# Gate values of a feed-forward layer, rounded and subtracted by single blocks or by pairs, beside block-sparse attention on one core

## The chip, the cores and the metric

The kernel runs on one core of a Trainium2 chip. The metric is the time of one execution in device microseconds (us); less is better. The engines work in parallel, each through its own instructions in a fixed order: TensorE (PE, matmuls into PSUM banks), VectorE (DVE), ScalarE (ACT), GpSimd (POOL) and SyncE (SP, which here issues nearly all DMA transfers).

## The reference

Attention with a block mask over 4 batches of 8 heads (768 positions, 64 columns a head), then a feed-forward layer with a piecewise gate, all in fp32:

```
scores = scale * q @ k.T                     # (B, H, S, S), masked to -1e9 outside chosen 32x32 blocks
attn   = softmax(scores) ;  a = attn @ v
x = a.transpose(0, 2, 1, 3).reshape(3072, 512)
h = x @ w_in                                 # 512 -> 2048
g = where(h >= 1, h, where(h <= -1, 0, (h + 1)**2 / 4))
out = g @ w_out                              # 2048 -> 512
```

## The kernel before

**Numbers.** Matmuls run on values in a rounded format (F32R). For near fp32 accuracy an operand is split into a rounded part "hi" and the rest "lo" = value - hi, and a product is made of three matmuls: hi*hi, hi*lo, lo*hi. So each gate value `r` needs a rounding cast (`gh`, on ACT) and a subtraction (`gl`, on DVE).

**Attention.** Each head works through scores (L318, L319), exponentials (L323, ACT), their rounding `ph` (L196, ACT) and rest `pl` (L331, DVE), and the products with v (L350, L351). Beside these run the row maxima of the next head (L267 on PE, L272 on DVE).

**Feed-forward.** `moe` works on half a batch: 384 positions, 16 blocks of 128 hidden columns (`fi`). For a block, the first layer makes 12 matmuls of 384 columns into one PSUM bank (L472 to L474, three for each of four slices `j`). The gate chain follows: relu(h/2 + 1/2) on ACT (L478), square on ACT (L481), `max(min(r, 1), h)` on DVE (L484, the last reader of the bank), the cast `gh` on ACT (L196, a helper for all roundings) and the subtraction `gl` on DVE (L493). The second layer makes three groups of three matmuls of 512 columns into the banks `oa0` to `oa2` (L500, L501 with `gh`, L502 with `gl`). The weights of the second layer come by SP, a tile `w` of 512 KB for each block, in three buffers.

The first-layer bank is `hp`, one buffer, so a block's first L472 waits until the block before has been read by L484. Only in the last batch do odd blocks use a bank of `pa` (three buffers, shared with the scores and maxima). Batch b's feed-forward runs beside the attention of batch b + 1; the last batch's runs alone, from about 830 us. In the first half batch the weights of the second layer are still converted from 64-bit numbers on ACT and DVE.

**Order.** Each step is put on a list with a planned time, `at(t, function, ...)`, where the offsets come from tables (`G["gr"]`, `G["gh"]`, `G["l2"]` ...) and `p` is the planned time of a block. The list is sorted, and a scheduler makes of it the final order of each engine. It lets work that it believes ready go ahead of work that stands earlier in the list, so the order that results is not read from the planned times alone. On the chip each engine keeps that order.

Of the kernel before, what the change touches and what calls it, by code (L numbers as in the profile page):

```python
# [8 lines left out]
F32 = mybir.dt.float32  # L9
F32R = mybir.dt.float32r  # L10
# [3 lines left out]
ALU = mybir.AluOpType  # L14
# [7 lines left out]
HALF = 384  # L22
DM, FF = 512, 2048
NF = FF // 128
# [13 lines left out]
def body(ctx, tc, qk_t, v, sampled_blocks, moe_w_in, moe_w_out, ind, cm, negd, ident, fold, out):  # L38
    nc = tc.nc
# [10 lines left out]
    mt = pool("mt", 2)  # L50
    op = pool("op", 1)
# [21 lines left out]
    def f(ap):  # L73
        return ap.bitcast(F32)
# [54 lines left out]
    def at(t, fn, *args):  # L129
        plan.append((t, fn, args))  # L130
# [26 lines left out]
    def convert(t, src, dst, done=None):  # L157
        st = {}

        def load():  # L160
            st["raw"] = cv.tile([128, 512, 2], I32, name="raw", bufs=3)
            Q_RAW.dma_start(out=st["raw"], in_=src.bitcast(I32).rearrange("p (c w) -> p c w", w=2))

        def bits():
            raw = st["raw"]
            lo32, hi32 = raw[:, :, 0], raw[:, :, 1]
            a = st["a"] = cv.tile([128, 512], I32, name="cva", bufs=2)
            nc.scalar.activation(out=f(a), in_=f(hi32), func=AF.Abs)
            nc.vector.tensor_scalar(out=f(a), in0=f(a), scalar1=CLO, scalar2=CHI, op0=ALU.max, op1=ALU.min)
            nc.vector.tensor_scalar(out=a, in0=a, scalar1=3, scalar2=0x3FFFFFFF,  # L170
                                    op0=ALU.logical_shift_left, op1=ALU.bitwise_and)
            nc.vector.scalar_tensor_tensor(out=a, in0=hi32, scalar=-0x40000000, in1=a,
                                           op0=ALU.bitwise_and, op1=ALU.bitwise_or)
            nc.vector.scalar_tensor_tensor(out=a, in0=lo32, scalar=29, in1=a,
                                           op0=ALU.logical_shift_right, op1=ALU.bitwise_or)

        def split():
            hi, lo = dst()
            rounded(CH, hi, f(st["a"]))
            nc.vector.tensor_tensor(out=lo, in0=f(st["a"]), in1=f(hi), op=ALU.subtract)  # L180
            if done:
                done()

        conv.append((t, load, bits, split))
# [5 lines left out]
    def rounded(eng, dst, src):  # L190
        if eng is nc.vector:
            eng.tensor_copy(out=dst, in_=src)
        elif eng is nc.gpsimd:
            eng.tensor_scalar(out=dst, in0=src, scalar1=1.0, scalar2=0.0, op0=ALU.mult, op1=ALU.add)
        else:
            eng.copy(out=dst, in_=src)  # L196
# [252 lines left out]
    def moe(t0, p, b, hf, first):  # L449

        g = {}
        G = {**P, **PM} if first else P

        def w_load(fi):
            w = g["w", fi] = wst.tile([128, 2, DM], F32R, name="w")
            Q_W.dma_start(out=f(w.rearrange("p a d -> p (a d)")), in_=f(wo_dram[fi]))

        def w_dst(fi):
            w = g["w", fi] = wst.tile([128, 2, DM], F32R, name="w")
            return w[:, 0], w[:, 1]  # L460

        def w_keep(fi):
            Q_KEEP.dma_start(out=f(wo_dram[fi]), in_=f(g["w", fi].rearrange("p a d -> p (a d)")))

        def l1(fi, j):
            if j == 0:
                last = b == B - 1 and fi % 2
                g["h", fi] = psa.tile([128, 512], F32, name="pa") if last else psh.tile([128, 512], F32, name="hp")
            hv = g["h", fi][:, 0:HALF]
            x = xt[b, j, hf]  # L470
            fs = slice(fi * 128, (fi + 1) * 128)
            nc.tensor.matmul(out=hv, lhsT=wi[:, j, 0, fs], rhs=x[:, 0], start=(j == 0), stop=False)  # L472
            nc.tensor.matmul(out=hv, lhsT=wi[:, j, 0, fs], rhs=x[:, 1], start=False, stop=False)  # L473
            nc.tensor.matmul(out=hv, lhsT=wi[:, j, 1, fs], rhs=x[:, 0], start=False, stop=(j == NP - 1))  # L474

        def g_relu(fi):
            r = g["r", fi] = mt.tile([128, HALF], F32, name="r")
            nc.scalar.activation(out=r, in_=g["h", fi][:, 0:HALF], func=AF.Relu, bias=half_c, scale=0.5)  # L478

        def g_sq(fi):  # L480
            nc.scalar.activation(out=g["r", fi], in_=g["r", fi], func=AF.Square)  # L481

        def g_max(fi):
            nc.vector.scalar_tensor_tensor(out=g["r", fi], in0=g["r", fi], scalar=1.0, in1=g["h", fi][:, 0:HALF],  # L484
                                           op0=ALU.min, op1=ALU.max)

        def g_hi(fi):
            gh = g["gh", fi] = mt.tile([128, HALF], F32R, name="gh", bufs=3)
            rounded(nc.scalar, gh, g["r", fi])

        def g_lo(fi):
            gl = g["gl", fi] = mt.tile([128, HALF], F32R, name="gl", bufs=3)
            (nc.gpsimd if first and fi % 4 in GL1 else nc.vector).tensor_tensor(out=gl, in0=g["r", fi], in1=f(g["gh", fi]), op=ALU.subtract)  # L493

        def l2(fi, t):
            if fi == 0:
                g["o", t] = psc.tile([128, DM], F32, name=f"oa{t}")
            ts = slice(t * 128, (t + 1) * 128)
            gh, gl, w, o = g["gh", fi], g["gl", fi], g["w", fi], g["o", t]
            nc.tensor.matmul(out=o, lhsT=gh[:, ts], rhs=w[:, 0], start=(fi == 0), stop=False)  # L500
            nc.tensor.matmul(out=o, lhsT=gh[:, ts], rhs=w[:, 1], start=False, stop=False)  # L501
            nc.tensor.matmul(out=o, lhsT=gl[:, ts], rhs=w[:, 0], start=False, stop=(fi == NF - 1))  # L502

        end = b == B - 1 and hf == 1
        dst = out[b * S:(b + 1) * S].rearrange("(p t) m -> p t m", t=T)

        def o_copy(t):
            if t == 0:
                g["out"] = op.tile([128, 3, DM], F32, name="o")
            if end and t == 1:  # L510
                nc.vector.tensor_copy(out=g["out"][:, t], in_=g["o", t])
            else:
                nc.scalar.copy(out=g["out"][:, t], in_=g["o", t])
            if end:
                Q_OUT.dma_start(out=dst[:, hf * 3 + t], in_=g["out"][:, t])

        def o_store():
            if not end:
                Q_OUT.dma_start(out=dst[:, hf * 3:hf * 3 + 3], in_=g["out"])

        for fi in range(NF):
            u = t0 + fi * p
            if first:
                convert(u + 1.5 * p - P["co"], moe_w_out[fi * 128:(fi + 1) * 128, :], lambda fi=fi: w_dst(fi),
                        lambda fi=fi: w_keep(fi))
            else:
                at(u - p, w_load, fi)
            for j in range(NP):
                at(u + j * p * G["l1"], l1, fi, j)
            m = u + p / 2  # L530
            at(m + G["gr"], g_relu, fi)
            at(m + G["gs"], g_sq, fi)
            at(m + G["gm"], g_max, fi)
            at(m + G["gh"], g_hi, fi)
            at(m + G["gl"], g_lo, fi)
            for t in range(3):
                at(u + G["l2"] * p + t * p * G["l3"], l2, fi, t)
        for t in range(3):
            at(t0 + (NF + G["l2"] - 1) * p + (t + 1) * p * G["l3"] + 0.05, o_copy, t)
        at(t0 + (NF + 1) * p + 0.1, o_store)  # L540


    at(TC, consts)
# [6 lines left out]
    p = PER * H / (2 * NF)  # L550
    for b in range(NMOE):
        for hf in range(2):
            moe(begin[b] + hf * NF * p, p, b, hf, b == 0 and hf == 0)
# [25 lines left out]
GL1 = ()  # L579
# [64 lines left out]
```

## Time and profile before

| | us |
|---|---|
| median of 3 runs | 981.09 (981.05 to 982.55) |
| the profiled execution | 980.94 |
| its span, first to last instruction | 979.0 |
| PE busy in the span | 945.3 (97%) |
| DVE busy | 736.8 (75%) |
| ACT busy | 646.3 (66%) |
| POOL busy | 251.5 (26%) |

The rows of the prediction come from this execution. A row of a timeline gives the start, the duration, engine, line and operation, the tile written and the tiles read, the shape, and in brackets the idle time before it with what ended it. A matmul is shown from its start to the end of its last result; the next starts well before that end, so the distance between two starts is the price of one. A row of waits gives who waited for whom, the sum in us, how many times, and the longest. A row by stage gives the stretch, its length, the busy time (and number) of PE, weight loads, DVE, ACT and POOL, the granted clock, the DMA share and GB/s. A row of one tile gives the minimum, median and maximum duration in ns.

### The profile page before, as it was taken

The page shows a single profiled execution, that of the slowest core. Times are in us where ns is not written, and L with a number is a line of the kernel's source. Part 1 is how long each engine was busy: PE and PEld are TensorE (multiplying, and loading weights), DVE is VectorE, ACT ScalarE, POOL GpSimd, SP SyncE. Part 2 cuts the span into 40 slices and gives each one's busy share as a digit, 9 for nine tenths or more (in the row PEclk, how much of TensorE's full clock was granted, in tenths as well). Part 3 has the DMA queues.
Part 4 walks back from the last instruction along what each step waited for, and adds up shares of the span by engine and source line. Part 5 has one row for each costly group of instructions (what it writes and reads, how often), then busy time and mean ns, then how long its engine had stood idle before and what let it go on. Part 6 is the DMA issues. An engine that isn't in the chain of part 4 may idle for free.

```text
span 979.0 us, 14671 instructions
## 1 busy us (share of the span) xinstructions
PE 945.3 (97%) x4746; PEld 833.3 (85%) x4746; DVE 736.8 (75%) x1390; ACT 646.3 (66%) x1326; POOL 251.5 (26%) x229
## 2 busy tenths in 40 slices
PE   5898999999899999999999999999999999999998
PEld 3676677888789999998999899999999999899997
DVE  5897988779998888988888888888788885422222
ACT  4686787677677676767677667776767676433433
POOL 1000000013334443433434343433434343000000
PEclk9899999999999999999999999999999999999999
DMA  6756766754364544545556453646445442433442
GB/s 193 227 155 183 200 201 214 259 173 140 129 205 144 146 148 136 178 135 154 158 154 189 118 153 120 198 138 176 137 143 178 126 114 89 154 129 129 161 129 97
DMA packets 56216, 154.44 MB, mean 158 GB/s; under 512 B 9612, under 2 KB 17952, under 8 KB 56140
## 3 DMA queue, kind: packets, MB, share of 16 engines
q1 hardware_dynamic: 56100, 153.48, 52.0%
q8 instruction: 38, 0.62, 0.3%
q14 instruction: 38, 0.31, 0.1%
q10 hardware_dynamic: 40, 0.03, 0.0%
HBM read 100.92 MB, written 14.81 MB: 118 GB/s over the span
## 4 chain that ended last, share of the span: by engine, by line
PE 88%; DVE 5%; ACT 3%; DMA 2%; issue 2%; SPq 0%; ACTq 0%; DVEq 0%
PE oa L500 8%; PE oa L502 8%; PE oa L501 8%; PE hp L472 8%; PE hp L474 8%; PE hp L473 8%; PE pa L267 7%; PE pa L318 5%; PE pa L319 5%; PE po L350 5%; PE po L348 5%; PE po L351 4%; PE oa L348 3%; DVE mc L272 1%; PE oa L318 1%
## 5 line engine op out<-in xcount | busy, mean ns | idle before, releaser
L338 POOL TENSOR_TENSOR acc<-acc,pt 128x384 f32<-128x384 f32 x176 | 202.2, 1149 | 226.2 <-ACT pt L323 190.3
L272 DVE TENSOR_REDUCE mc<-pa 128x1 f32<-128x384 f32 x384 | 202.8, 548 | 24.1 <-PE pa L267 21.0
L196 ACT CAST ph<-pt 128x384 fp32r<-128x384 f32 x264 | 135.7, 514 | 88.2 <-PE po L350 84.5
L331 DVE TENSOR_TENSOR pl<-pt,ph 128x384 fp32r<-128x384 f32 x264 | 166.3, 630 | 35.6 <-ACT ph L196 34.9
L323 ACT ACTIVATE pt<-pa 128x384 f32<-128x384 f32 x288 | 140.6, 489 | 50.8 <-PE pa L319 42.0
L472 PE MATMUL hp<-x,wi 128*128 128x384 f32 x448 | 155.0, 346 | 2.9 <-DVE r L484 2.9
L500 PE MATMUL oa<-w,gh 128*128 128x512 f32 x384 | 153.6, 400 | 0.3 <-ACT gh L196 0.3
L502 PE MATMUL oa<-w,gl 128*128 128x512 f32 x384 | 151.4, 394 | 0.0
L473 PE MATMUL hp<-x,wi 128*128 128x384 f32 x448 | 151.4, 338 | 0.0
L474 PE MATMUL hp<-x,wi 128*128 128x384 f32 x448 | 151.2, 338 | 0.0
L501 PE MATMUL oa<-w,gh 128*128 128x512 f32 x384 | 150.8, 393 | 0.0
L267 PE MATMUL pa<-KA,QA 88*128 88x384 f32 x384 | 138.8, 381 | 5.3 <-DMA QA<-qkh 3.0
L338 POOL TENSOR_TENSOR acc<-pt 128x384 f32<-128x384 f32 x44 | 45.8, 1040 | 349.4 <-ACT pt L323 349.4
L484 DVE SCALAR_TENSOR_TENSOR r<-r,hp 128x384 f32<-128x384 f32 x112 | 61.7, 551 | 74.0 <-ACT r L481 73.6
L493 DVE TENSOR_TENSOR gl<-r,gh 128x384 fp32r<-128x384 f32 x128 | 83.7, 654 | 23.4 <-ACT gh L196 22.9
L478 ACT ACTIVATE r<-hp,half_c 128x384 f32<-128x384 f32 x112 | 65.1, 582 | 53.4 <-PE hp L474 50.3
L318 PE MATMUL pa<-QA,KA 102*128 102x384 f32 x288 | 99.3, 345 | 0.8 <-ACT pt L323 0.4
L319 PE MATMUL pa<-QB,KB 128*128 128x384 f32 x288 | 97.9, 340 | 0.0
L267 PEld LDWEIGHTS pa<-KA,QA 88*128 88x128 f32 x384 | 73.2, 192 | 27.8 <-DVE mc L272 6.7
L350 PE MATMUL po<-ph,vn 128*128 128x384 f32 x264 | 91.5, 347 | 2.3 <-DVE xun L360 1.9
L472 PEld LDWEIGHTS hp<-x,wi 128*128 128x128 f32 x448 | 84.5, 189 | 8.6 <-DVE r L484 4.2
L351 PE MATMUL po<-pl,vn 128*128 128x384 f32 x264 | 88.6, 336 | 0.0
(100 smaller groups left out, 1634.1 us busy)
## 6 DMA issues: line engine op xcount, KB each, us to landing
w<-wo_dram SPq DMA_DIRECT2D x112, 512.0 KB
qk<-in_qk_t_dram SPq DMA_DIRECT2D x32, 384.0 KB
raw<-in_moe_w_in_dram SPq DMA_DIRECT2D x16, 512.0 KB
raw<-in_moe_w_out_dram SPq DMA_DIRECT2D x16, 512.0 KB
wo_dram<-w SPq DMA_DIRECT2D x16, 512.0 KB
lv<-in_v_dram SPq DMA_DIRECT2D x32, 192.0 KB
KA<-qkh SPq DMA_DIRECT2D x32, 192.0 KB
QA<-qkh SPq DMA_DIRECT2D x32, 192.0 KB
```

Source lines behind the costliest of these rows:

```text
L267: nc.tensor.matmul(out=pm[:, 0:HALF], lhsT=QAi[0:KM, t * 128:(t + 1) * 128], rhs=KAi[0:KM, kh * HALF:(kh + 1) * HALF], start=True, stop=True)
L272: nc.vector.reduce_max(out=st["mc"][:, t, kh:kh + 1], in_=st.pop(("pm", t, kh))[:, 0:HALF], axis=AX.X)
L318: nc.tensor.matmul(out=ps[:, 0:HALF], lhsT=KAi[0:KA, ks], rhs=QAi[0:KA, cs], start=True, stop=False)
L319: nc.tensor.matmul(out=ps[:, 0:HALF], lhsT=st["KB"][:, ks], rhs=st["QB"][:, cs], start=False, stop=True)
L331: (nc.gpsimd if i < 2 * H and c in PL1 else nc.vector).tensor_tensor(out=pl, in0=st["p", c], in1=f(st["ph", c]), op=ALU.subtract)
L338: nc.gpsimd.tensor_tensor(out=st["acc", hf], in0=prev, in1=st["p", c], op=ALU.add)
L472: nc.tensor.matmul(out=hv, lhsT=wi[:, j, 0, fs], rhs=x[:, 0], start=(j == 0), stop=False)
L473: nc.tensor.matmul(out=hv, lhsT=wi[:, j, 0, fs], rhs=x[:, 1], start=False, stop=False)
L474: nc.tensor.matmul(out=hv, lhsT=wi[:, j, 1, fs], rhs=x[:, 0], start=False, stop=(j == NP - 1))
L500: nc.tensor.matmul(out=o, lhsT=gh[:, ts], rhs=w[:, 0], start=(fi == 0), stop=False)
L501: nc.tensor.matmul(out=o, lhsT=gh[:, ts], rhs=w[:, 1], start=False, stop=False)
L502: nc.tensor.matmul(out=o, lhsT=gl[:, ts], rhs=w[:, 0], start=False, stop=(fi == NF - 1))
```

## The change

Two neighbouring blocks, 2n and 2n + 1, share one tile `r` of 2 x 384 columns. Relu, square and max stay as they are, a block each. The cast `gh` and the subtraction `gl` are made once for the pair, over 768 columns, after the odd block's max. The second-layer matmuls are planned later: by 0.6 p for the even block and 0.2 p for the odd one, so that both stand close together behind the pair's cast. `r`, `gh` and `gl` have two buffers of pairs each; before, `r` had two and `gh` and `gl` three single ones. The copies and the store of the output are planned 0.2 p later. In the new file L500 to L502 are L504 to L506, L478 is L480, L481 is L483, L484 is L486 and L493 is L496.

```diff
         def g_relu(fi):
-            r = g["r", fi] = mt.tile([128, HALF], F32, name="r")
+            if fi % 2 == 0:
+                g["rr", fi // 2] = mt.tile([128, 2, HALF], F32, name="r")
+            r = g["r", fi] = g["rr", fi // 2][:, fi % 2]
             nc.scalar.activation(out=r, in_=g["h", fi][:, 0:HALF], func=AF.Relu, bias=half_c, scale=0.5)
...
-        def g_hi(fi):
-            gh = g["gh", fi] = mt.tile([128, HALF], F32R, name="gh", bufs=3)
-            rounded(nc.scalar, gh, g["r", fi])
-
-        def g_lo(fi):
-            gl = g["gl", fi] = mt.tile([128, HALF], F32R, name="gl", bufs=3)
-            (nc.gpsimd if first and fi % 4 in GL1 else nc.vector).tensor_tensor(out=gl, in0=g["r", fi], in1=f(g["gh", fi]), op=ALU.subtract)
+        def g_hi(fp):
+            gh = g["ghp", fp] = mt.tile([128, 2, HALF], F32R, name="gh")
+            rounded(nc.scalar, gh, g["rr", fp])
+            g["gh", 2 * fp], g["gh", 2 * fp + 1] = gh[:, 0], gh[:, 1]
+
+        def g_lo(fp):
+            gl = mt.tile([128, 2, HALF], F32R, name="gl")
+            nc.vector.tensor_tensor(out=gl, in0=g["rr", fp], in1=f(g["ghp", fp]), op=ALU.subtract)
+            g["gl", 2 * fp], g["gl", 2 * fp + 1] = gl[:, 0], gl[:, 1]
...
-            at(m + G["gh"], g_hi, fi)
-            at(m + G["gl"], g_lo, fi)
+            if fi % 2:
+                at(m + G["gh"], g_hi, fi // 2)
+                at(m + G["gl"] + 0.1, g_lo, fi // 2)
+            w = u + G["l2"] * p + (0.6 * p if fi % 2 == 0 else 0.2 * p)
             for t in range(3):
-                at(u + G["l2"] * p + t * p * G["l3"], l2, fi, t)
+                at(w + t * p * G["l3"], l2, fi, t)
         for t in range(3):
-            at(t0 + (NF + G["l2"] - 1) * p + (t + 1) * p * G["l3"] + 0.05, o_copy, t)
-        at(t0 + (NF + 1) * p + 0.1, o_store)
+            at(t0 + (NF + G["l2"] - 0.8) * p + (t + 1) * p * G["l3"] + 0.05, o_copy, t)
+        at(t0 + (NF + 1.2) * p + 0.1, o_store)
```

`GL1` is empty in this kernel, so all subtractions `gl` are on DVE in both. How the final orders differ is shown at three places.

PE beside attention, third batch: what follows the last first-layer matmul of an odd block (its bank is `hp_8815` before and `hp_8613` now). Before:

```order
L474 MATMUL hp_8815<-x_7433,wi_119 128x384
L318 MATMUL pa_8845<-QA0_113,KA0_115 128x384
L319 MATMUL pa_8845<-QB_8545,KB_8544 128x384
L500 MATMUL oa0_7610<-w_8642,gh_8803 128x512
L501 MATMUL oa0_7610<-w_8642,gh_8803 128x512
L502 MATMUL oa0_7610<-w_8642,gl_8809 128x512
L350 MATMUL po_8727<-ph_8805,vn_8159 128x384
L351 MATMUL po_8727<-pl_8807,vn_8159 128x384
L500 MATMUL oa1_7630<-w_8642,gh_8803 128x512
L501 MATMUL oa1_7630<-w_8642,gh_8803 128x512
L502 MATMUL oa1_7630<-w_8642,gl_8809 128x512
L318 MATMUL pa_8878<-QA0_113,KA0_115 128x384
```

Now:

```order
L474 MATMUL hp_8613<-x_7267,wi_119 128x384
L318 MATMUL pa_8646<-QA0_113,KA0_115 128x384
L319 MATMUL pa_8646<-QB_8346,KB_8345 128x384
L350 MATMUL po_8521<-ph_8602,vn_7973 128x384
L351 MATMUL po_8521<-pl_8607,vn_7973 128x384
L318 MATMUL pa_8672<-QA0_113,KA0_115 128x384
L319 MATMUL pa_8672<-QB_8346,KB_8345 128x384
L378 MATMUL pa_8679<-sel_111,psum_8330 24x32
L318 MATMUL pa_8711<-QA0_113,KA0_115 128x384
L319 MATMUL pa_8711<-QB_8346,KB_8345 128x384
L472 MATMUL hp_8696<-x_5366,wi_119 128x384
L473 MATMUL hp_8696<-x_5366,wi_119 128x384
```

The second layer of the block before (`gh_8803`), which stood here, is gone: it belongs to this block's pair now. The next block's L472 on `hp` comes after 9 matmuls, before after 18; the second layer of the block itself after 15, before after 39. Through this stage four kinds of pair repeat. From the odd block's last L474 to the next L472 there are 8 matmuls of 384 columns and one L378; 11; 9; 9 and one L378. To the pair's first L504 there are 14 and one L378; 18; 15; 16 and one L378. Before, these distances were 15 to 22 and 35 to 43.

ACT at the same place, from the relu of the odd block to its cast. Before:

```order
L478 ACTIVATE r_8853<-hp_8815,half_c_112 128x384
L323 ACTIVATE pt_8861<-pa_8845 128x384
L481 ACTIVATE r_8853<-r_8853 128x384
L196 CAST ph_8890<-pt_8861 128x384
L355 COPY otmp_8869<-po_8727 64x384
L196 CAST vn_8875<-lv_8741 128x6x64
L196 CAST gh_8886<-r_8853 128x384
```

Now:

```order
L480 ACTIVATE r_8585<-hp_8613,half_c_112 128x384
L323 ACTIVATE pt_8658<-pa_8646 128x384
L483 ACTIVATE r_8585<-r_8585 128x384
L355 COPY otmp_8663<-po_8521 64x384
L196 CAST vn_8669<-lv_8537 128x6x64
L196 CAST gh_8677<-r_8585 128x768
```

The cast has 768 columns and one operation less ahead of it; in two of the four kinds of pair the operations between the square and the cast are otmp, a `ph` and an exponential, one more than here.

PE at the very end of the program, from the last first-layer matmul of block 15. Before:

```order
L474 MATMUL pa_11252<-x_10305,wi_119 128x384
L500 MATMUL oa0_10816<-w_11192,gh_11248 128x512
L501 MATMUL oa0_10816<-w_11192,gh_11248 128x512
L502 MATMUL oa0_10816<-w_11192,gl_11250 128x512
L500 MATMUL oa1_10824<-w_11192,gh_11248 128x512
L501 MATMUL oa1_10824<-w_11192,gh_11248 128x512
L502 MATMUL oa1_10824<-w_11192,gl_11250 128x512
L500 MATMUL oa2_10828<-w_11192,gh_11248 128x512
L501 MATMUL oa2_10828<-w_11192,gh_11248 128x512
L502 MATMUL oa2_10828<-w_11192,gl_11250 128x512
L500 MATMUL oa0_10816<-w_11224,gh_11278 128x512
```

Now:

```order
L473 MATMUL pa_10930<-x_10052,wi_119 128x384
L474 MATMUL pa_10930<-x_10052,wi_119 128x384
L504 MATMUL oa0_10545<-w_10875,gh_10949 128x512
L505 MATMUL oa0_10545<-w_10875,gh_10949 128x512
L504 MATMUL oa1_10555<-w_10875,gh_10949 128x512
```

Block 14's nine matmuls stood between block 15's first layer and its second; now both blocks need `gh_10949`, which is made after that L474. In the rest of the last batch 16 first-layer matmuls stand between an odd block's last L474 and its pair's first L504 (21 matmuls before, from each block's L474 to its own L500).

## The prediction

> **What bounds the kernel now.** I read the page's busy shares, then the windows by stage, the chain, what TensorE (PE) waits for, and last the timeline at the places where the change moves matmuls.
>
> ```profile
> span 979.0 us, 14671 instructions
> PE 945.3 (97%) x4746; PEld 833.3 (85%) x4746; DVE 736.8 (75%) x1390; ACT 646.3 (66%) x1326; POOL 251.5 (26%) x229
> PE 88%; DVE 5%; ACT 3%; DMA 2%; issue 2%; SPq 0%; ACTq 0%; DVEq 0%
> ...
> 200.00:250.00 50.00, 46.67 (x236) 40.31 (x237) 44.50 (x76) 37.57 (x78) 15.96 (x14) 1.00 0.53 172
> 250.00:300.00 50.00, 46.07 (x238) 40.43 (x237) 48.99 (x90) 34.05 (x72) 18.58 (x16) 1.00 0.47 156
> 300.00:830.00 530.00, 527.55 (x2775) 485.91 (x2774) 438.00 (x819) 376.43 (x786) 211.97 (x190) 1.00 0.51 148
> ```
>
> PE is the bound: the chain is 88% PE, and from 300 to 830 us PE is idle for 2.5 us of 530 while VectorE (DVE) has 92 and ScalarE (ACT) 154 us free. So time taken off DVE or ACT cannot shorten that stretch, and any new hole on PE lengthens it one for one. Only at 200 to 300 us is there something to win: PE idles 3.3 + 3.9 us while DVE is nearly full. What PE waits for on the gate path today:
>
> ```profile
> PE hp L472 <- DVE r L484: 2.9, 2, 2.0
> PE oa L500 <- ACT gh L196: 0.3, 1, 0.3
> ```
>
> **Why it hardly waits.** One block beside attention: its last first-layer matmul (L474), the gate chain on ACT and DVE, the next block's first matmul into the one `hp` bank (L472 at 563.30) and the second-layer matmul (L500 at 566.98) that uses this block's gate value (the CAST gh at 562.36).
>
> ```profile
> 559.25 0.34 PE L474 MATMUL hp<-x,wi 128*128 128x384 f32 x1
> 559.43 0.34 PE L318 MATMUL pa<-QA,KA 102*128 102x384 f32 x1
> 562.34 0.40 PE L502 MATMUL oa<-w,gl 128*128 128x512 f32 x1
> 562.67 0.24 PE L378 MATMUL pa<-sel,psum 128*24 128x32 f32 x2
> 562.84 0.45 PE L350 MATMUL po<-ph,vn 128*128 128x384 f32 x1
> 563.30 0.34 PE L472 MATMUL hp<-x,wi 128*128 128x384 f32 x1
> 566.98 0.40 PE L500 MATMUL oa<-w,gh 128*128 128x512 f32 x1
> ...
> 559.63 0.58 ACT L478 ACTIVATE r<-hp,half_c 128x384 f32<-128x384 f32 x1
> 560.48 0.53 ACT L481 ACTIVATE r<-r 128x384 f32<-128x384 f32 x1
> 560.91 0.52 ACT L196 CAST ph<-pt 128x384 fp32r<-128x384 f32 x1
> 561.45 0.47 ACT L355 COPY otmp<-po 64x384 f32<-64x384 f32 x1
> 561.94 0.51 ACT L196 CAST vn<-lv 128x384 fp32r<-128x384 f32 x1
> 562.36 0.51 ACT L196 CAST gh<-r 128x384 fp32r<-128x384 f32 x1
> ...
> 561.03 0.55 DVE L484 SCALAR_TENSOR_TENSOR r<-r,hp 128x384 f32<-128x384 f32 x1 [0.70 <-ACT r L481]
> ```
>
> Count from 559.43, where PE goes on after the last L474. The max on DVE ends at 561.58, 2.15 us later, and frees `hp`; the next block wants it at 563.30, a slack of 1.72. The cast ends at 562.87, 3.44 later; PE wants it at 566.98, a slack of 4.11. On ACT each further operation starts 0.42 to 0.54 after the one before. 384-column matmuls follow at 0.17 us (559.25 to 559.43).
>
> **The change, step by step.** Half of the rounding casts and subtractions go, the other half grow to 768 columns.
>
> ```profile
> L196 ACT CAST gh<-r 128x384 fp32r<-128x384 f32 x128 | 65.6, 513 | 29.0 <-DVE r L484 28.5
> L196 ACT CAST qkh<-qk x32: 816/834/853, 3.9 to 764.2; 128x768 fp32r<-128x768 f32 x32
> L493 DVE TENSOR_TENSOR gl<-r,gh x128: 507/552/1392, 166.2 to 972.6; 128x384 fp32r<-128x384 f32 x128
> L228 DVE TENSOR_TENSOR qk<-qk,qkh x32: 881/953/1766, 8.7 to 768.9; 128x768 f32<-128x768 f32 x32
> ```
>
> The same operations at 768 columns exist in the trace (minimum, median, maximum). ACT saves 64 x (2 x 0.513 - 0.834) = 12.3 us, DVE 64 x (2 x 0.552 - 0.953) = 9.7 us by medians. Both lie beside PE work; I count them as 0 in the sum, with the 7.3 us of PE idle at 200 to 300 us as the most they could give. The price of a pair's chain is that the cast is 0.32 us longer and the subtraction 0.40.
>
> *The stage beside attention.* By the orders above, after the odd block's last L474 the next first-layer block follows `hp` after 9 to 11 matmuls instead of 15 to 22, and the pair's first second-layer matmul after 15 to 18 instead of 35 to 43, in four kinds of pair that repeat. In time, at 0.174 each and 0.17 for L378, L472 is reached at 1.56, 1.91, 1.57 and 1.74 us. The bank is free at 2.15 + 0.05 = 2.20 (the 0.05 is the step from a producer's end to PE in the last fence below). PE stands 0.64, 0.29, 0.63 and 0.46, mean 0.5. The second layer is reached, unstalled, at 2.61, 3.13, 2.61 and 2.95. Its cast is the second operation behind otmp in two kinds (square at 1.05, otmp 1.48, vn 1.97, cast 2.39, end 3.22, PE 3.27) and one further back in the others (2.85, end 3.68, PE 3.73). That is 0.66, 0.60, 0.66 and 0.78 late, mean 0.68, the first stall included since it lies on the same stretch of PE. A stopped stream restarts with 0.11 lost (below). So 0.78 a pair, and 40 such pairs: 31 us. Low end: the bank alone, 0.5 x 40 = 20. High end: the chain one 768-column cast (0.83) longer by the ACT queue, where copies of `o` or qkh stand ahead, in two pairs of three: 53. The cover that is gone is the second layer of the block before, which stood between and is now itself waiting.
>
> The subtraction starts behind the cast, in one kind of pair behind one more 0.55 of DVE, and takes 0.95; its first user stands 6 to 10 matmuls behind the first L504, 1.1 us or more: 0, ends 0 and 0.3 a pair. The odd square, max and both relus are unchanged. A weight tile `w` is freed later by the shift of the second layer and its load, issued on SP, later too; behind it on SP stand the next head's moves:
>
> ```profile
> SPq L456 <- PE oa L502: 118.4, 32, 6.5
> PE pa L267 <- DMA QA<-qkh: 3.0, 2, 2.1
> ```
>
> SP already waits for L502 and PE has paid 3.0 us for moves in two places. I take 0; one such wait more in every fourth head would be 6 x 1.5 = 9, which is in the range.
>
> *The first eight pairs (163 to 275 us)* have the weight conversions in the DVE queue, and the max can be very late:
>
> ```profile
> 218.78 0.34 PE L474 MATMUL hp<-x,wi 128*128 128x384 f32 x1
> 223.35 0.53 DVE L484 SCALAR_TENSOR_TENSOR r<-r,hp 128x384 f32<-128x384 f32 x1
> ```
>
> Here it ends 4.93 after PE went on at 218.95, so a bank wanted at 1.6 would cost 3.4. On the other side DVE itself limits this stretch, so PE's holes may only change place. I take the middle stage's 0.78: 6 us; ends 0 and 4 x 3.4 = 14.
>
> *The last batch alone (14 pairs).* Here the banks alternate and PE never stops today. The last block's chain shows the price with nothing else in the queues:
>
> ```profile
> 969.97 0.34 PE L474 MATMUL pa<-x,wi 128*128 128x384 f32 x1
> 970.14 0.40 PE L500 MATMUL oa<-w,gh 128*128 128x512 f32 x1
> 970.38 0.39 PE L501 MATMUL oa<-w,gh 128*128 128x512 f32 x1
> 971.99 0.39 PE L502 MATMUL oa<-w,gl 128*128 128x512 f32 x1
> 972.66 0.50 PE L500 MATMUL oa<-w,gh 128*128 128x512 f32 x1 [0.28 <-ACT gh L196]
> 973.01 0.40 PE L501 MATMUL oa<-w,gh 128*128 128x512 f32 x1
> 972.10 0.51 ACT L196 CAST gh<-r 128x384 fp32r<-128x384 f32 x1 [0.62 <-DVE r L484]
> ```
>
> From 970.14 to the cast's end 2.47, to PE 2.52; with 0.32 more, 2.84. The new order has 16 first-layer matmuls there, 16 x 0.174 = 2.78. So 0.06 plus the restart (0.35 instead of 0.24 to the next) 0.11: 0.17 x 14 = 2.4; ends 0 and 0.3 x 14 = 4.2.
>
> *The end.* Block 14's nine matmuls no longer cover block 15's chain. Now PE stands 0.44 (972.66 against 971.99 + 0.23), then 2.84: +2.4.
>
> Sum: 31 + 6 + 2.4 + 2.4 = 42 on the span of 979.0; the profiled execution took 980.94, 1.94 beside its span, and the median of the three runs is 981.09. So 1023 us.
>
> **A rule against the change.** The block at 559.43 shows that PE does not pass over a waiting matmul: `hp` was free at 561.58, but L472 started at 563.30, behind L502, L378 and L350, as it stands in the program. The Trainium skill, "TensorE: Matmul & The Clock Gate", Part 2, says that the engine pulls weight loads ahead but keeps matmuls in program order; by it every wait above stops all that stands behind, and the middle stage costs its 31 us. If ready attention matmuls could pass, that term would be 0 and the sum 992. The trace agrees with the rule, as far as this one place tells.
>
> **Rivals.** (a) *The middle finds its cover.* If ACT and DVE, lighter by 22 us in all, run the chain 0.7 us sooner, only the tail and the end are left: 981 + 2.4 + 2.4 = 986. Against it: relu, square and max are not shortened, and the bank waits for these alone. 0.10. (b) *The queues make it worse.* Max and cast stand behind more work when PE stops and ACT and DVE bunch up, or moves behind `w` on SP come late: 53 + 14 + 4 + 2 = 73, so from 1042 up to 1054. For it: the late max at 223.35. 0.13. (c) *Faster*: DVE's saving at 200 to 300 us removes the idle 7.3 us there and the waits stay hidden: 974, or 978 with half of it. It decides if the max ends within 1.56 us of the last L474, against the 2.15 measured, which is why I give it 0.05. (d) *No change*, gains and holes cancelling within 2 us (0.2% is about what runs of this kernel can tell from nothing): 0.04.
>
> **Numbers.** The forecast of 1023 has 0.68; its own bounds are 1003 (20 + 0 + 0 + 2 = 22) and 1042, where it passes into (b). The range that leaves out most of (a), (c) and (d) and the far part of (b) is 1000 to 1046. Slower: 0.68 + 0.10 + 0.13 = 0.91; same 0.04; faster 0.05.
>
> **What would show it.** PE idle between 300 and 830 us of about 30 us instead of 2.5, under the waits of L472 for the max and L504 for the cast, tens of times each, most under a microsecond; the 64 casts at 0.83 and subtractions at 0.95 to 1.1; in the last batch short stops before L504, and one of near 3 us before the last pair. Wrong would be: few such waits, or waits for something not named here, such as the moves of the next head.

## The result: 4.4% slower, and the profile after

| | before | after |
|---|---|---|
| median, us | 981.07 (978.23 to 982.55, 6 runs) | 1024.99 (1020.48 to 1027.26, 6 runs) |
| ratio | | 1.0444, 95% interval 1.0416 to 1.0473 |
| span of the profiled execution | 979.0 | 1023.7 |

The prediction was 1023 (1000 to 1046). First the page of the changed kernel (span, busy shares, the chain that ended last) and the window of the stage beside attention, which now lasts to 860 us:

```profile
span 1023.7 us, 14484 instructions
PE 974.9 (95%) x4746; PEld 829.5 (81%) x4746; DVE 742.8 (73%) x1326; ACT 637.5 (62%) x1262; POOL 259.4 (25%) x229
PE 77%; ACT 9%; DVE 8%; DMA 3%; issue 3%; SPq 0%; ACTq 0%; DVEq 0%
...
300.00:860.00 560.00, 544.86 (x2756) 478.31 (x2755) 447.10 (x774) 368.08 (x740) 217.71 (x188) 1.00 0.49 139
```

PE makes the same 4746 matmuls. Its share of the chain fell from 88 to 77%, and ACT and DVE have 17% of it instead of 8. From 300 us on PE is idle 15.1 us of 560, before 2.5 of 530. What PE waits for on the gate path, and at the scores' bank:

```profile
PE hp L472 <- DVE r L486: 7.4, 21, 0.6
PE pa L318 <- ACT pt L323: 5.6, 8, 1.2
...
PE oa L504 <- ACT gh L196: 2.9, 2, 2.7
...
PE pa L267 <- ACT pt L323: 2.8, 3, 1.3
PE pa L267 <- DMA QA<-qkh: 2.0, 2, 1.2
```

And before, at the scores' banks:

```profile
PE pa L267 <- ACT pt L323: 1.2, 3, 0.5
...
PE pa L318 <- ACT pt L323: 0.4, 1, 0.4
```

L472 waits 21 times for the max, where it did so twice before. L318 and L267 wait 11 times for an exponential that frees a bank of `pa`, 8.4 us in all, before 4 times and 1.6 us. L504 shows only 2 waits for the cast, one of them 2.7 us long, at the end of the program. These sums do not make up the loss, and the reason is in the timeline of one pair, after the odd block's last L474:

```profile
788.29 0.34 PE L474 MATMUL hp<-x,wi 128*128 128x384 f32 x1
788.47 0.34 PE L318 MATMUL pa<-QA,KA 102*128 102x384 f32 x1
789.90 0.33 PE L267 MATMUL pa<-KA,QA 88*128 88x384 f32 x1
790.69 0.44 PE L472 MATMUL hp<-x,wi 128*128 128x384 f32 x1 [0.46 <-DVE r L486]
790.97 0.34 PE L473 MATMUL hp<-x,wi 128*128 128x384 f32 x1
791.83 0.41 PE L504 MATMUL oa<-w,gh 128*128 128x512 f32 x1
...
790.08 0.56 DVE L486 SCALAR_TENSOR_TENSOR r<-r,hp 128x384 f32<-128x384 f32 x1 [0.95 <-ACT r L483]
790.86 0.84 ACT L196 CAST gh<-r 128x768 fp32r<-128x768 f32 x1
```

L472 could have started at 789.90 + 0.174 = 790.07 and did at 790.69, when the max was done: 0.62 us. The row gives 0.46 idle, because the matmul ahead counts as busy to its modelled end, 790.23, though the next could have started at 790.07. The next matmul then comes 0.28 later instead of 0.17. So this stop cost 0.73 and shows as 0.46, and a hold under 0.17 shows as nothing. A pair's loss is therefore read from starts: from the matmul behind one odd block's last L474 to that behind another, four pairs later, it is 517.58 to 574.00 before and 774.25 to 833.80 after. That is 56.42 and 59.55, so 3.13 more, 0.78 a pair.

The end of the program, and the granted clock there (the number ahead of the last two):

```profile
1010.78 0.34 PE L474 MATMUL pa<-x,wi 128*128 128x384 f32 x1
1013.79 0.60 PE L504 MATMUL oa<-w,gh 128*128 128x512 f32 x1 [2.67 <-ACT gh L196]
1014.19 0.63 PE L505 MATMUL oa<-w,gh 128*128 128x512 f32 x1
1014.62 0.63 PE L504 MATMUL oa<-w,gh 128*128 128x512 f32 x1
...
1017.54 0.40 PE L504 MATMUL oa<-w,gh 128*128 128x512 f32 x1
```

```profile
1014.00:1016.00 2.00, 2.00 (x6) 1.50 (x6) 0.73 (x1) 0.00 (x0) 0.00 (x0) 0.51 0.00 0
1016.00:1018.00 2.00, 2.00 (x7) 1.59 (x6) 0.00 (x0) 0.00 (x0) 0.00 (x0) 0.63 0.00 0
1018.00:1020.00 2.00, 1.75 (x8) 1.13 (x6) 0.69 (x1) 0.80 (x2) 0.00 (x0) 1.00 0.06 23
```

PE stands from 1010.95 to 1013.79, 2.84 us. Then matmuls of 512 columns come mostly at 0.42 to 0.43 us instead of 0.23 until 1017.5, at a granted clock of 0.51 and 0.63 on average in the two stretches.

Where the time went, from the start of the last L474 of each odd block, after minus before:

| stage | predicted, us | measured, us |
|---|---|---|
| first eight pairs | 6 | 3.3 |
| 40 pairs beside attention | 31 | 34.4 |
| last batch alone | 2.4 | 3.1 |
| the end | 2.4 | 3.8 |
| sum | 42 | 44.6 |

### The profile page after: what moved, and what is told of

The parts are those of the page before. It is cut to its first block, busy times and chain, and to the rows that moved or that the text cites. A ratio compares the mean times of both kernels' runs of the same rounds, so it can differ in the third digit from the quotient of the medians.

```text
span 1023.7 us, 14484 instructions
## 1 busy us (share of the span) xinstructions
PE 974.9 (95%) x4746; PEld 829.5 (81%) x4746; DVE 742.8 (73%) x1326; ACT 637.5 (62%) x1262; POOL 259.4 (25%) x229
## 4 chain that ended last, share of the span: by engine, by line
PE 77%; ACT 9%; DVE 8%; DMA 3%; issue 3%; SPq 0%; ACTq 0%; DVEq 0%
PE oa L506 8%; PE oa L504 8%; PE oa L505 8%; PE hp L472 7%; PE hp L474 7%; PE hp L473 6%; PE pa L267 5%; PE po L348 4%; PE po L350 3%; PE po L351 3%; PE pa L318 3%; PE pa L319 3%; PE oa L348 3%; DVE pl L331 2%; ACT pt L323 2%
## 5 line engine op out<-in xcount | busy, mean ns | idle before, releaser
L338 POOL TENSOR_TENSOR acc<-acc,pt 128x384 f32<-128x384 f32 x176 | 207.0, 1176 | 251.6 <-ACT pt L323 249.8
L272 DVE TENSOR_REDUCE mc<-pa 128x1 f32<-128x384 f32 x384 | 198.9, 549 | 27.6 <-PE pa L267 25.2
L331 DVE TENSOR_TENSOR pl<-pt,ph 128x384 fp32r<-128x384 f32 x264 | 169.7, 645 | 33.4 <-ACT ph L196 28.0
L472 PE MATMUL hp<-x,wi 128*128 128x384 f32 x448 | 158.7, 354 | 7.6 <-DVE r L486 7.4
L504 PE MATMUL oa<-w,gh 128*128 128x512 f32 x384 | 156.3, 407 | 3.4 <-ACT gh L196 2.9
L505 PE MATMUL oa<-w,gh 128*128 128x512 f32 x384 | 152.0, 396 | 0.0
L473 PE MATMUL hp<-x,wi 128*128 128x384 f32 x448 | 151.6, 338 | 0.0
L506 PE MATMUL oa<-w,gl 128*128 128x512 f32 x384 | 149.9, 402 | 1.2 <-DVE gl L496 0.3
L474 PE MATMUL hp<-x,wi 128*128 128x384 f32 x448 | 150.9, 337 | 0.0
L267 PE MATMUL pa<-KA,QA 88*128 88x384 f32 x384 | 138.2, 388 | 9.2 <-ACT pt L323 2.8
L338 POOL TENSOR_TENSOR acc<-pt 128x384 f32<-128x384 f32 x44 | 48.8, 1110 | 352.3 <-ACT pt L323 352.3
L318 PE MATMUL pa<-QA,KA 102*128 102x384 f32 x288 | 102.6, 356 | 6.3 <-ACT pt L323 5.6
L267 PEld LDWEIGHTS pa<-KA,QA 88*128 88x128 f32 x384 | 73.1, 192 | 36.8 <-ACT pt L323 12.5
L472 PEld LDWEIGHTS hp<-x,wi 128*128 128x128 f32 x448 | 84.7, 189 | 21.9 <-DVE r L486 16.6
L350 PE MATMUL po<-ph,vn 128*128 128x384 f32 x264 | 89.6, 339 | 1.1 <-ACT xun L368 1.1
L506 PEld LDWEIGHTS oa<-w,gl 128*128 128x128 f32 x384 | 71.1, 189 | 23.5 <-DVE gl L496 10.1
L504 PEld LDWEIGHTS oa<-w,gh 128*128 128x128 f32 x384 | 72.7, 189 | 18.7 <-ACT gh L196 12.4
L473 PEld LDWEIGHTS hp<-x,wi 128*128 128x128 f32 x448 | 84.7, 189 | 2.7
```

The source lines that it names most:

```text
L267: nc.tensor.matmul(out=pm[:, 0:HALF], lhsT=QAi[0:KM, t * 128:(t + 1) * 128], rhs=KAi[0:KM, kh * HALF:(kh + 1) * HALF], start=True, stop=True)
L272: nc.vector.reduce_max(out=st["mc"][:, t, kh:kh + 1], in_=st.pop(("pm", t, kh))[:, 0:HALF], axis=AX.X)
L331: (nc.gpsimd if i < 2 * H and c in PL1 else nc.vector).tensor_tensor(out=pl, in0=st["p", c], in1=f(st["ph", c]), op=ALU.subtract)
L338: nc.gpsimd.tensor_tensor(out=st["acc", hf], in0=prev, in1=st["p", c], op=ALU.add)
```

## The experiments

Two theories stood against each other. The order theory is the prediction's: PE reaches the bank and the pair's cast too early. The queue theory is rival (b)'s second half: tiles `w` come free later and hold SP, with the moves behind it. Each ratio is to the kernel before, timed beside it on the same chip.

**1. Pairs, everything behind them 1.0 p later.** The second layer, the loads and conversions of `w`, the copies and the store.

```diff
-            w = u + G["l2"] * p + (0.6 * p if fi % 2 == 0 else 0.2 * p)
+            w = u + G["l2"] * p + 1.0 * p
...
```

> Pairs as in the change, but the second layer of both blocks is planned a whole block period p later than in the kernel before (1.0 p instead of 0.6 p and 0.2 p), with its weight loads, conversions, copies and store; the order that comes of it has the second layer of the pair before standing behind the odd block again: PE time to the next use of hp 3.1 to 4.1 us beside attention (2.1 at one place), to the pair's second layer 5.2 us or more, 4.2 us in the last batch, 2.1 us at the very end. Order theory (the loss is PE reaching the bank and the cast too early): the holes close, 978 to 984 us, ratio 0.997 to 1.003, PE idle from 300 us to the last batch under 5 us. Rival (the 768-column operations, or second layers close together, cost by themselves, for instance through DVE or the w loads): both are still there, so 1010 us or more.

989.41 us, ratio 1.0084 (1.0070 to 1.0098). Four fifths of the loss are gone with the pairs kept, but the last 8 us were not expected. In the profiled execution, 8.3 us longer than the one before, the 40 pairs beside attention lose 8.8 us, the end 2.2, and the stretch ahead of them gains 2.8. What PE waits for:

```profile
PE po L350 <- DVE xun L360: 5.5, 12, 0.9
...
PE hp L472 <- DVE r L486: 3.1, 4, 1.4
```

L472 waits for the gate's bank 4 times instead of 21, but L350 now waits 12 times for the single bank `po` of attention and its reader, before 3 times. A place that the order theory did not name now stops.

**2. Single casts at the change's later times.** The kernel before with the second layer, copies and store where the change plans them.

```diff
-                at(u + G["l2"] * p + t * p * G["l3"], l2, fi, t)
+                at(u + G["l2"] * p + (0.6 * p if fi % 2 == 0 else 0.2 * p) + t * p * G["l3"], l2, fi, t)
...
```

> The kernel before with single casts and subtractions, and only the planned times of the second layer as in the change (0.6 p and 0.2 p later), so the second layers of two blocks stand close together. In the order that comes of it the second layer stands 7.6 us of PE time or more behind its own block, and the next use of hp 2.2 to 4.3 us. Order theory: 978 to 985 us, since the cast is long done and the bank, free at 2.2, is wanted at 2.2 in one block of four and later in the others. Rival (closeness, or w tiles that come free late, is the cost): 1000 us or more.

991.08, ratio 1.0101 (1.0086 to 1.0116): between the two expectations. The later times alone, without a pair, cost 10 us in an order that the planner makes anew. SP waits longer than before (118.4 for L502 and 59.0 at L397):

```profile
SPq L456 <- PE oa L502: 158.9, 49, 9.3
SPq L397 <- DVE rc L387: 142.5, 29, 9.1
```

**3 and 4. The chain shorter by the square.** `g_sq` left out of the changed kernel, and of the kernel before; so the gate lacks its square, and the chain one ACT operation of 0.53 a block.

```diff
-            at(m + G["gs"], g_sq, fi)
```

> The changed kernel with the square left out (that part of the gate is not computed), so the chain from the last first-layer matmul to the max and the cast is one ACT operation shorter, about 0.5 us. In the order that comes of it PE reaches hp after 1.4 to 1.6 us, the pair's second layer after 2.6 to 3.1, in the last batch after 2.3. Order theory: the bank is free near 1.65, the cast at PE near 2.8 to 3.3, so 0.2 to 0.3 us a pair instead of 0.8 and little in the last batch: 990 to 1002 us, against 1025 with the square. Rival (the loss is in the 768-column operations, the closeness or the loads): 1018 us or more.

> The kernel before with the square left out, as the measure for the run without square of the changed kernel. Both theories: no effect, 978 to 983 us, because ACT is not on PE's path there; 67 us of ACT work are gone.

Pairs: 1012.03, ratio 1.0314 (1.0296 to 1.0332). Before: 981.03, ratio 1.0004 (0.9989 to 1.0020). ACT's work as such costs nothing, but the length of the chain does once the pairs wait for it: 13 us, less than the 23 to 35 expected. L472 no longer waits for the max often (3 times, 1.2 us), but the subtraction is late (row below), and by starts L318 and L267 still stop for 18.1 us in the 40 pairs (19.9 in the changed kernel):

```profile
PE oa L506 <- DVE gl L496: 4.0, 9, 0.7
```

**5. The stop at the end filled.** 14 matmuls into a spare bank, read by nobody, between the last L474 and the pair's L504 (here L510; the added ones are L480).

```diff
...
+            if end and fi == NF - 1:
+                at(u + NP * p * G["l1"], spin)
```

> The changed kernel with 14 extra matmuls of 384 columns into a spare bank, whose result nobody reads, between the last first-layer matmul of the program and the pair's first L504: 14 x 0.174 = 2.4 us, inside the stop of 2.84 us that stands there. Clock theory: after this stop nine matmuls come at 0.42 to 0.43 us instead of 0.23 and the granted clock is 0.51 to 0.63, because PE stood; with the stop filled the clock stays at 1.00 and the nine come at 0.23, so the end gets 9 x 0.2 = 1.8 us shorter: 1023.2 against 1025.0, span about 1022. Rival: the nine are slow because of their operands (the pair's tiles, two operands from one tile) and not by the clock: spacing still 0.42, time unchanged at 1025.

1022.9, ratio 1.0432 (1.0406 to 1.0459). That interval overlaps with the change's own, so the trace has to decide:

```profile
1012.32 2.59 PE L480 MATMUL pa<-x,wi 128*128 128x384 f32 x14
1015.17 0.50 PE L510 MATMUL oa<-w,gh 128*128 128x512 f32 x1 [0.26 <-ACT gh L196]
1015.50 0.40 PE L511 MATMUL oa<-w,gh 128*128 128x512 f32 x1
```

```profile
1014.00:1016.00 2.00, 1.75 (x10) 1.30 (x9) 1.10 (x2) 0.83 (x1) 0.00 (x0) 1.00 0.00 0
1016.00:1018.00 2.00, 2.00 (x10) 1.66 (x9) 0.11 (x1) 0.00 (x0) 0.00 (x0) 1.00 0.00 0
```

The second layer starts 2.85 us after the last L474 could be followed, as without them. But the clock stays at 1.00, the matmuls come at 0.23, and from that start to the end of the program it takes 8.3 us instead of 9.9. So the clock's share of the end is 1.6 us. That the filling kept the clock up is not shown by this alone: the kernel of experiment 11 has the same stop unfilled, from 1019.75 to 1022.59, 2.84 us, and its clock stayed at 1.00 too:

```profile
1022.59 0.50 PE L504 MATMUL oa<-w,gh 128*128 128x512 f32 x1 [2.68 <-ACT gh L196]
1022.93 0.39 PE L505 MATMUL oa<-w,gh 128*128 128x512 f32 x1
...
1022.00:1024.00 2.00, 1.41 (x6) 1.19 (x7) 0.96 (x1) 0.54 (x1) 0.00 (x0) 1.00 0.00 0
```

From the first L504 to the start of the last L506 it takes 3.99 us there, 3.98 with the stop filled, and 5.58 in the changed kernel.

**6, 7 and 11. A fourth buffer for `w`.** In the kernels of 2, of 1, and in the changed kernel.

```diff
-    wst = pool("wst", 3)
+    wst = pool("wst", 4)
```

> The kernel before with the later times of the second layer, copies and store (as in the run with single casts, 991.1), and four buffers of w instead of three, so that a later second layer holds no load of w on SP. Queue theory: the 10 us of that run came from SP, which stood longer for the release of w (158.9 us of waits for L502, 142.5 for rc) with den and the moves of the next head behind it; with the fourth buffer the wait for L502 falls below 30 us and the time returns to 979 to 984. Rival: the 10 us come from the order on PE itself (the second layer's nine matmuls stand at a place where they hold the scores and the maxima): still 987 to 993, with the SP wait gone.

> The pairs with the second layer 1.0 p later for both blocks (as in the run that took 989.4), and four buffers of w. Queue theory: what was left there (8 us, waits of L350 for xun and of L267 for the moves) came from late loads and moves on SP: 978 to 983. Order theory: what was left are the holes of the pair's longer chain and the bank: 986 to 990, and SP's waits alone get shorter.

> The changed kernel with four buffers of w instead of three. Queue theory: about 10 of its 44 us come from SP, which waits for the release of w by L506 (176.9 us) with den and the moves behind it: 1012 to 1018. Order theory (bank, cast, subtraction and the scores' banks reached too early on PE make up all of it): 1022 to 1027.

Single casts at the later times: 985.78, ratio 1.0047 (1.0028 to 1.0065), half of the 10 us back. Pairs 1.0 p later: 988.50, ratio 1.0084 (1.0064 to 1.0105), no change. The changed kernel: 1033.62, ratio 1.0544 (1.0519 to 1.0569), 9 us worse. The buffer also made the planner reorder all engines but POOL, so none of the three is a change of one thing. Nor did it take SP's wait away. In the changed kernel the wait fell from 176.9 us to

```profile
SPq L456 <- PE oa L506: 130.1, 36, 10.2
```

while that at L397 rose from 134.2 to 155.5. With single casts it fell from 158.9 to 139.4 and L397 rose from 142.5 to 161.5; at 1.0 p it stayed (123.8 and 122.1). So these runs do not decide about the queue theory, and for single casts at the later times it stays open. For the pairs other rows speak against it: PE's own waits for the moves `QA<-qkh` are 2.0 us in the changed kernel and were 3.0 before, and the version of the pairs that loses least, experiment 10, has a longer wait on SP than the change:

```profile
SPq L456 <- PE oa L506: 230.6, 63, 7.9
```

Of what the changed kernel got worse, 5 us are stops of L506 for the subtraction, read by starts in the 40 pairs; why was not separated from the new order.

**8. The odd blocks in another bank.** They use a bank of `pa` in all batches, so no L472 waits for an odd block's max in `hp`.

```diff
-                last = b == B - 1 and fi % 2
+                last = fi % 2
```

> The changed kernel with the odd blocks' first layer in a bank of pa in all batches, so that the next block no longer waits for the odd block's max in hp; by the order PE then reaches the pair's first L504 after 2.9 to 3.6 us of matmuls, against 2.6 to 3.1 before. Prediction's reckoning (the pair's cast sets the loss, the bank's stop is contained in it): the cast reaches PE at 3.27 to 3.9, late by 0.3 to 0.5 a pair with the restart, 12 to 20 us in the middle; with 3 + 3 + 4 elsewhere 1001 to 1011. Rival 1, the bank makes the loss and the cast adds little: 985 to 995. Rival 2, the odd blocks take the bank from the scores and exponentials: PE waits at L318 for L323 instead, 1020 and more.

1012.43, ratio 1.0325 (1.0300 to 1.0350). This is just above the range by the prediction's reckoning; the bank is not all of the loss, and L318 did not take it over. The 40 pairs beside attention lose 20.3 us instead of 34.4, so 14.1, 0.35 a pair, came with the bank. By starts PE stops 0.40 us a pair up to the pair's first L504, where it was 0.93 in the change and 0.3 to 0.5 was expected if the cast sets the loss. What was not expected is behind it, 0.38 instead of 0.21, and shows at the subtraction:

```profile
PE oa L506 <- DVE gl L496: 4.5, 10, 1.1
...
PE oa L504 <- ACT gh L196: 2.7, 1, 2.7
```

**9. Single casts, everything 1.0 p later.** Experiment 1 without the pairs (and four buffers of `gh` and `gl`).

> The kernel before (single casts and subtractions) with the second layer, the loads of w, the conversions, the copies and the store 1.0 p later, as in the pairs that took 989.4, and four buffers of gh and gl. By the order its distances to hp and po are those of the kernel before (3.1 to 4.3 and 1.8 to 2.0 us). Pairing theory: the 8 us left there come from the pair's operations of 768 columns (cast 0.83, subtraction 0.95), which stand ahead of otmp, xun and the max in the queues of ACT and DVE: with single ones 979 to 983. Rival: they come from the lag alone (later w, longer store): 986 to 990.

981.12, ratio 1.0009 (0.9996 to 1.0022): nothing lost. A lag of a whole block is free with single casts; so the 8 us of experiment 1 come only with the pairs, or with the order that the planner made for them. L350 waits here as seldom as before:

```profile
PE po L350 <- DVE xun L360: 2.7, 4, 0.9
```

Which of the pair's operations makes `xun` late in experiment 1, or whether it is only its place in DVE's order, the runs do not tell.

**10 and 12. Pairs with lags of 1.2 p and 0.8 p.**

> The pairs with the second layer 1.2 p later for both blocks instead of 1.0 p. By the order PE reaches po again after 1.9 to 2.4 us (1.8 to 2.1 at 1.0 p), hp after 2.4 to 3.4 (3.1 to 4.1) and the pair's first L504 after 7.6. Cover theory (PE waits where the next user of a single bank is nearer than its readers need, 2.2 for hp and about 2.2 for po): the 5.5 us of waits of L350 for xun fall to 1 to 3, hp gives back up to 2: 983 to 988. Rival (the remainder is the size of the pair's operations, wherever the second layer stands): 988 to 991.

> The pairs with the second layer 0.8 p later for both blocks (0.6 p and 0.2 p in the change, 1.0 p in the run that took 989.4). By the order PE reaches the pair's first L504 after 5.2 to 5.7 us (the cast is there at 3.3 to 3.9), hp after 2.4 to 3.1 (free at 2.2) and po after 1.7 to 2.1. Cover theory: all of the gate chain is covered again, so nearly the same as at 1.0 p, po a little worse: 988 to 995. Rival (the loss falls gradually with the lag): about halfway, 1000 to 1010.

| lag of the even and odd block | us | ratio |
|---|---|---|
| 0.6 p and 0.2 p (the change) | 1024.99 | 1.0444 (1.0416 to 1.0473) |
| 0.8 p | 1005.58 | 1.0247 (1.0222 to 1.0272) |
| 1.0 p | 989.41 | 1.0084 (1.0070 to 1.0098) |
| 1.2 p | 985.62 | 1.0048 (1.0031 to 1.0065) |

At 1.2 p the waits of L350 for `xun` at L360 are gone and half of the remaining 8 us came back, as the cover theory expected. At 0.8 p it missed by 10 us, and the time lies where the rival (the loss falls gradually with the lag) had it: the pair's first L504 beside attention starts 5.3 to 7.5 us after PE went on behind the odd block's last L474, no longer waits for the cast except at the end, and 25 us are lost all the same. The largest part shows at the bank:

```profile
PE hp L472 <- DVE r L486: 10.5, 10, 1.6
...
PE oa L504 <- ACT gh L196: 1.3, 1, 1.3
```

```profile
640.59 1.56 DVE L228 TENSOR_TENSOR qk<-qk,qkh 128x768 f32<-128x768 f32 x1
642.08 0.54 DVE L486 SCALAR_TENSOR_TENSOR r<-r,hp 128x384 f32<-128x384 f32 x1
642.67 0.44 PE L472 MATMUL hp<-x,wi 128*128 128x384 f32 x1 [0.94 <-DVE r L486]
```

In this order the max of one pair in four stands behind the 1.3 to 1.6 us of L228 on DVE and ends 3.8 to 4.6 us after PE went on, instead of 2.2 to 2.6 (the rows are of an execution with a span of 1000.1). In that execution the 40 pairs lose 18.4 us, and L472 with its restarts has 10.7 of them. Distances on PE, counted from the order, told nothing of that; the reader's own queue sets the other side. No version is faster than the kernel before.

## Why the prediction was right, point by point

**The bound.** Right. PE bounds the stage, and holes in it cost one for one. Of the savings counted as 0, ACT's busy time did fall, by 8.8 us (12.3 predicted). The group of subtractions on DVE fell from 83.7 to 67.1 us, yet DVE's busy time rose by 6.0: L276, an operation of 128x6 that mostly stands right behind the subtraction, took 20.6 us in all instead of 5.0 (median 0.97 instead of 0.15), and the rest is less overlap; why was not looked into. Leaving out all squares of the kernel before bought no time either.

**The stage beside attention.** The term was 0.78 a pair and the four pairs at 774 us show 0.78; the 40 pairs together 0.86, since a few lose 1 us more where the relu comes 1.2 to 1.5 us late (pairs at 578 and 758 us). A stop is counted here as the part of the distance between two starts that is beyond the usual one for these two shapes, the median of both traces:

| stops of PE, us a pair | predicted | four pairs | 40 pairs |
|---|---|---|---|
| up to the pair's first L504, restart included | 0.78 | 0.81 | 0.93 |
| behind it | 0 | 0.27 | 0.21 |
| stops that the kernel before has | 0 | 0.30 | 0.28 |
| loss: the first two less the third | 0.78 | 0.78 | 0.86 |

The first row bears the mechanism out. The cast ends 3.2 to 3.9 us after PE went on in 36 of the 40 pairs (3.22 or 3.68 predicted), and the first L504 starts 0.05 to 0.06 behind it in 21, as here, where the cast ends at 778.08. In the others it comes 0.13 us behind it or more, because PE had been held elsewhere.

```profile
777.26 0.82 ACT L196 CAST gh<-r 128x768 fp32r<-128x768 f32 x1
...
777.74 0.34 PE L473 MATMUL hp<-x,wi 128*128 128x384 f32 x1
778.14 0.50 PE L504 MATMUL oa<-w,gh 128*128 128x512 f32 x1
...
778.71 0.34 PE L474 MATMUL hp<-x,wi 128*128 128x384 f32 x1
```

So the cast sets the loss and the stops ahead of it are part of its lateness, and experiment 8 fits that. Experiment 3 shows the limit: with the cast earlier PE still stops 0.62 us a pair up to the first L504, where 0.2 to 0.3 was expected, so there other stops hold it. Where PE stops on the way was only half foreseen. In the 40 pairs, before and now, with restarts: L472 2.5 and 13.8 us, L504 0 and 4.2, L506 0 and 4.5, but L318 and L267 together 3.4 and 19.9. The three banks of `pa` for scores and maxima lost the same cover, and the exponential that frees one stands behind the gate's work on ACT: at 579.90 it follows the relu of 579.43, and L318 starts at 580.43, when it is done. The prediction does not name these banks.

The step that failed is "the subtraction ... 0, ends 0 and 0.3 a pair": it costs 0.11 a pair (0.14 in the four), and with the scores' banks 0.21 behind the first L504. The sum also took off nothing for the 0.28 a pair that the kernel before already stops there. These two nearly cancel, so that the term came out so near is in part luck. A small misreading is L378, counted at 0.17: from 562.34 to 562.67 the row shows 0.33 where 0.23 is usual, so it is 0.27 in all. The cover named in the prediction is the right one: put the second layer one block back (experiment 1), and L472 stops 2.7 us in the 40 pairs and L318 with L267 3.4, about as before.

**The first eight pairs.** 3.3 instead of 6, within the ends 0 and 14.

**The last batch.** 3.1 instead of 2.4. The term was 0.17 a pair for 14 pairs; 0.18 to 0.22 was measured, over 15: L504 comes 2.84 to 2.85 us after the odd block's last L474 could be followed, the predicted chain to the hundredth, and PE has 2.78 of matmuls there.

**The end.** The stop is 2.84 as predicted. The term was 2.4, for the stop alone; what it lacked is the halved clock after it, 1.6 us by experiments 5 and 11. That makes 4.0, and 3.8 was measured.

**The rivals.** (a), the middle finds its cover: 34.4 us there say no, and for the reason given, since the bank waits for relu, square and max, which did not get shorter. (b): its bunching shows as late relus in a few pairs only; its SP part is not borne out for the pairs (experiment 10, and PE's own waits for the moves). (c) asked for a max within 1.56 us: it ends at 2.16 to 2.28. (d) is excluded by the interval.

**The rule.** In the rows above L504 stands for the cast until 778.14, and L474, of a group in `hp` that L472 and L473 had begun, waits for nothing else that the trace shows and still comes behind it, at 778.71. So matmuls kept their place, as the Trainium skill, "TensorE: Matmul & The Clock Gate", Part 2, has it.

**The marker.** "PE idle of about 30 us" between 300 and 830 was wrong: 14.8, and 15.1 up to 860. A stop of 0.73 shows as 0.46, and small ones as nothing. The 64 casts at 0.83 and subtractions at 0.96 (medians) came as expected, and the one stop near 3 us before the last pair too.

## What to carry to other kernels

Matmuls that stand between a producer and its user are the cover of every single-buffered bank along that stretch: before two blocks are put together, count for each such bank when PE comes back to it and when its last reader ends, and look into the reader's own queue. If work is batched off the bound engine, move the users back by as much as the batch delays their inputs: that took the loss from 4.4% to 0.5%, and no gain was left to win, since the saved time lay on engines that did not bound. Read the price of short stops from the distance between starts, not from idle time.

## What the runs showed of the hardware that was not expected

A stop of 2.84 us was enough to halve the clock, and it stayed so for 3.4 us:

```profile
1014.05:1017.45 3.40, 3.40 (x9) 2.61 (x9) 0.68 (x1) 0.00 (x0) 0.00 (x0) 0.50 0.00 0
```

The length of the stop does not decide it alone: the same 2.84 us halved the clock at the end of experiment 8 as well, but not at the end of experiment 11. Earlier in the run of the changed kernel two shorter stops, with one matmul between them, went ahead of another such stretch:

```profile
248.37 0.45 PE L267 MATMUL pa<-KA,QA 88*128 88x384 f32 x1 [1.34 <-ACT pt L323]
249.80 0.69 PE L267 MATMUL pa<-KA,QA 88*128 88x384 f32 x1 [0.98 <-ACT pt L323]
250.28 0.52 PE L472 MATMUL hp<-x,wi 128*128 128x384 f32 x1
250.60 0.52 PE L473 MATMUL hp<-x,wi 128*128 128x384 f32 x1
```

```profile
250.00:252.00 2.00, 2.00 (x7) 2.00 (x8) 1.87 (x4) 1.68 (x4) 1.18 (x2) 0.50 1.02 347
```

Matmuls of 384 columns come at 0.32 instead of 0.17 there. The Trainium skill, "TensorE: Matmul & The Clock Gate", Part 1, says that the clock is gated to half after at least one idle window of about 3.4 us and comes back after about as long a busy one. The length of the slow stretch agrees (3.4 us); the stop does not have to last a whole window, since 2.84 us sufficed, though not in every execution.
